# Token mixer products over the whole array, one bank at a time, in an attention and mixer kernel

## The chip, the cores and the metric

The kernel runs on one core of one Trainium2 chip. The metric is the device time of one execution in microseconds (us); lower is better. A measurement is the median of several executions.

## The reference

Eight batches of causal attention with a decay (8 heads, 576 positions, 64 values per head), whose output feeds a token mixer (two products along the positions) and a channel mixer (two products along the 512 channels), each with a ReLU between and with the input added back:

```python
decay = cum[:, :, :, None] - cum[:, :, None, :]          # cum = cumsum(log(f))
scores = np.where(causal, -1e9, q @ k.T / 8 + decay)
x = softmax(scores) @ v                                  # [8, 576, 512]
h = np.maximum(x.transpose(0, 2, 1) @ w_tok1, 0.0) @ w_tok2   # w_tok1 [576, 256], w_tok2 [256, 576]
u = x + h.transpose(0, 2, 1)
out = u + np.maximum(u @ w_ch1, 0.0) @ w_ch2             # w_ch1 [512, 1536], w_ch2 [1536, 512]
```

The weights come in double precision and are decoded in the kernel. A factor is kept as a high and a low part (names ending in h and l, both fp32r), and a product is the sum of three: high by high, low by high, high by low.

## The kernel before

The program is a list of 4,680 steps. Each step is a group of instructions on one engine (PE has 940 of them), with the buffers that it needs. Tables of numbers (`ORDER`, one for each of PE, DVE, ACT, POOL and the DMA queue SP) say in which order an engine gets its steps. A planner replays them with costs for each step to give out buffers; the order of an engine is that of its table. All engines run in order and wait for each other with semaphores.

There are two stages. In the attention stage the 32 pairs of heads are worked through, and after each half of a batch (16 halves in all) the token mixer of that half. Meanwhile DVE, ACT and POOL decode the weights of the channel mixer, which go out to DRAM. The channel stage that follows is 2,520 matmuls in five chunks of two times 464 or 456 columns (`WIDE`), each over all 128 rows and columns of TensorE.

The attention stage uses TensorE in parts. Scores (L745, L751) and the products with v (L889, L892) run on 64 rows by 64 columns, four at a time side by side. Transposes (L860 of the probabilities, L1260 of the attention output) run on 64 rows by 128 columns, two side by side: even heads on the upper 64 rows, odd heads on the lower. PSUM has eight banks; two row halves never write into one bank at the same time.

The token mixer (`mixer`) of a half batch does, on PE: 20 transposes (L1260); two steps of the first product (`t1`, moving tiles of 256 columns); then for each of two groups of 128 channels two steps of the second product (`tok2`, moving tiles of 288 columns). ACT and DVE read the results out of the banks, take the ReLU and split into high and low (tiles `ring`), and DVE adds the second product to `xt`. The products are made by `joint`: a matmul over 128 rows is cut into two over 64 rows, which run side by side and write into two banks (L1243). Step (phase) 0 gives rows 0 to 63 to bank 0 and rows 64 to 127 to bank 1; phase 1 swaps the banks and adds the other half. Between the phases a `nop` on PE waits for the last matmuls of phase 0:

```python
for z in (0, 1):
    p.op("PE", [hm(width[0])] * n, lambda z=z: phase(z), rd=rd, wr=ps, bufs=[*ps, *extra], mode=1, ...)
```

So there are 96 such steps: 32 of the first product (14 pairs of matmuls, of which one may lack its second half) and 64 of the second (6 pairs). The names below: `xn`, `t1h`, `t1l`, `t2h`, `t2l` and `ring` are operands of these products, `pr` the probabilities, `ux`, `sg` and `wq` operands of the channel stage (L1045 to L1047 and L1126 to L1128).

A DMA of the attention stage is held back until an earlier one has landed (`run`, `hold`), so that the DMAs after that one, up to the last before it, amount to at least `AHEAD` in the planner's time (4,500, at 300 bytes a unit for most, 235 and 247 for some).

Of the kernel before, what the change touches and what calls it, by code (L numbers as in the profile page):

```python
# [15 lines left out]
P = 128  # L16
# [8 lines left out]
AHEAD, AHEAD_TO = 4500.0, 8  # L25
# [42 lines left out]
    ),  # L68
    DVE=(
# [193 lines left out]
class Plan:  # L263
# [48 lines left out]
    def run(self, slots):  # L312
# [6 lines left out]
        for k, o in enumerate(sent):  # L319
            if k > 1:  # L320
                ahead += sent[k - 1].lat
# [1212 lines left out]
```

## Time and profile before

| | |
|---|---|
| median of 3 executions | 933.82 us (933.11 to 934.39) |
| profiled execution | 933.73 us, span 931.9 us |
| PE busy | 911.5 us (98%), 10270 matmuls |
| DVE, ACT, POOL busy | 709.0, 523.0, 234.8 us |
| moved by DMA | 242.49 MB, 260 GB/s |
| granted TensorE clock | 0.999 |

The span goes from the first to the last instruction; the profiled execution took 1.8 us more. "Busy" of PE counts the time in which at least one matmul is on its way. Matmuls overlap, so a matmul's own duration is not what it costs; what it costs is the distance from its start to that of the next.

### The profile page before, as it was taken

How to read it: one execution, taken by the hardware profiler on the slowest of the kernel's cores; microseconds unless marked ns; L12 is line 12 of the kernel's file. 1: busy time of each engine (PE TensorE's matmuls, PEld its weight loads, DVE VectorE, ACT ScalarE, POOL GpSimd, SP SyncE). 2: the span in 40 equal slices, each digit the busy share in tenths (PEclk: the TensorE clock that was granted, in tenths of full speed). 3: DMA queues.
4: the chain of work that ended last, by engine and by line, in shares of the span. 5: the costliest groups of instructions: out<-in, count | busy, mean ns of one | idle time of the engine just before them, and what ended most of it. 6: DMA issues, size and time to landing. Idle time of an engine off the chain costs nothing.

```text
span 931.9 us, 26826 instructions
## 1 busy us (share of the span) xinstructions
PE 911.5 (98%) x10270; PEld 794.3 (85%) x10270; DVE 709.0 (76%) x1894; ACT 523.0 (56%) x1340; POOL 234.8 (25%) x320
## 2 busy tenths in 40 slices
PE   7999899999999999999999999999999999999998
PEld 5678788888788888988888888888889999999997
DVE  7988878888788778664898369953898359954786
ACT  6979888999888989721463135512353125421242
POOL 4577567676675662100000000000000000000000
PEclk9999999999999999999999999999999999999999
DMA  8989989899998988469799888898879878887774
GB/s 247 250 277 287 308 210 321 290 297 264 301 301 251 288 265 252 134 205 329 237 308 286 269 234 236 261 302 258 261 248 287 275 227 250 248 270 232 241 249 153
DMA packets 145023, 242.49 MB, mean 260 GB/s; under 512 B 19136, under 2 KB 76736, under 8 KB 144896
## 3 DMA queue, kind: packets, MB, share of 16 engines
q1 hardware_dynamic: 144800, 240.64, 84.0%
q8 instruction: 81, 1.33, 0.6%
q14 instruction: 46, 0.38, 0.1%
q10 hardware_dynamic: 96, 0.15, 0.0%
HBM read 199.52 MB, written 41.21 MB: 258 GB/s over the span
## 4 chain that ended last, share of the span: by engine, by line
PE 89%; DVE 6%; DMA 2%; ACT 2%; issue 2%; SPq 0%; DVEq 0%; ACTq 0%
PE bank L1243 11%; PE bank L1045 9%; PE bank L1126 9%; PE bank L1127 9%; PE bank L1128 9%; PE bank L1046 9%; PE bank L1047 9%; PE bank L745 7%; PE bank L889 7%; PE bank L860 5%; DVE pr L786 3%; PE bank L1260 1%; ACT pr L790 1%; DVE pf L868 1%; DMA d_raw<-in_w_tok 1%
## 5 line engine op out<-in xcount | busy, mean ns | idle before, releaser
L487 ACT ACTIVATE st<-H 128x464 fp32r<-128x464 f32 (+1 forms) x210 | 120.7, 587 | 117.4 <-PE bank L1127 78.1
L790 ACT ACTIVATE pr<-pr,nmin 128x192 f32<-128x192 f32 (+4 forms) x320 | 176.5, 558 | 15.2 <-DVE nmin L786 14.9
L1126 PE MATMUL bank<-st,wq 128*128 128x464 f32 (+1 forms) x420 | 156.0, 371 | 0.0
L1127 PE MATMUL bank<-st,wq 128*128 128x464 f32 (+1 forms) x420 | 155.9, 371 | 0.0
L1128 PE MATMUL bank<-st,wq 128*128 128x464 f32 (+1 forms) x420 | 155.7, 371 | 0.0
L786 DVE CUSTOM_DVE_ANT_0 pr<-bank,cb 128x448 f32<-128x448 f32 (+3 forms) x260 | 108.6, 458 | 11.3 <-PE bank L751 6.7
L745 PE MATMUL bank<-raw 64*64 64x448 f32 (+6 forms) x1408 | 111.4, 397 | 5.4 <-issue 1.8
L496 DVE TENSOR_TENSOR st<-H,st 128x464 fp32r<-128x464 f32 (+1 forms) x150 | 92.3, 631 | 13.4 <-ACT st L487 13.3
L981 DVE TENSOR_TENSOR tmp<-bank,tmp 128x464 f32<-128x464 f32 (+1 forms) x80 | 50.3, 633 | 61.6 <-PE bank L1047 46.6
L889 PE MATMUL bank<-pf,vr 64*64 64x128 f32 (+3 forms) x2048 | 96.5, 315 | 0.0
L870 ACT ACTIVATE pf<-bank 128x512 f32<-128x512 f32 x152 | 84.0, 595 | 11.8 <-PE bank L860 6.3
L1128 PEld LDWEIGHTS bank<-st,wq 128*128 128x128 f32 x420 | 78.8, 188 | 9.2
L1126 PEld LDWEIGHTS bank<-st,wq 128*128 128x128 f32 x420 | 78.9, 188 | 9.0
L1127 PEld LDWEIGHTS bank<-st,wq 128*128 128x128 f32 x420 | 78.8, 188 | 8.8
L889 PEld LDWEIGHTS bank<-pf,vr 64*64 64x64 f32 x2048 | 75.2, 133 | 7.7 <-ACT pf L870 1.5
L745 PEld LDWEIGHTS bank<-raw 64*64 64x64 f32 x1408 | 54.5, 133 | 31.7 <-issue 9.8
L1071 ACT ACTIVATE H<-bank 128x464 f32<-128x464 f32 (+1 forms) x30 | 16.5, 555 | 115.2 <-PE bank L1047 109.3
L860 PE MATMUL bank<-ident,pr 64*128 64x64 f32 x1536 | 63.6, 224 | 4.3 <-issue 1.4
L860 PEld LDWEIGHTS bank<-ident,pr 64*128 64x128 f32 x1536 | 58.9, 139 | 8.1 <-DVE nmin L786 2.2
L920 POOL TENSOR_TENSOR xt<-xt,rb 128x64 f32<-128x64 f32 (+1 forms) x64 | 52.4, 837 | 48.0 <-DMA rb<-recd 26.0
L790 ACT ACTIVATION_READ_ACCUMULATOR pr<-pr,nmin 128x1 f32 (+1 forms) x320 | 62.5, 195 | 0.0
L1243 PE MATMUL bank<-t2h,ring 64*128 64x288 f32 x512 | 60.7, 304 | 1.8 <-issue 1.5
(166 smaller groups left out, 2072.8 us busy)
## 6 DMA issues: line engine op xcount, KB each, us to landing
wq<-wd SPq DMA_DIRECT2D x420, 256.0 KB
raw<-in_qk SPq DMA_DIRECT2D x32, 576.0 KB
cb<-decd SPq DMA_DIRECT2D x26, 576.0 KB
d_raw<-in_w_ch SPq DMA_DIRECT2D x48, 256.0 KB
wd<-sg SPq DMA_DIRECT2D x24, 512.0 KB
vr<-in_v SPq DMA_DIRECT2D x64, 160.0 KB
rb<-recd SPq DMA_DIRECT2D x32, 320.0 KB
wd<-sg SPq DMA_DIRECT2D x24, 384.0 KB
```

The costliest lines, as they stand in the source:

```text
L487: nc.scalar.activation(out, in_, func, scale=scale)
L496: nc.vector.tensor_tensor(out, in_, asf(hi), op=ALU.subtract)
L745: nc.tensor.matmul(at(buf)[HALF[h], of : of + n], q[:, i0 : i0 + D], k[:, j0 : j0 + n], start=t not in (0, 1), stop=not nd, skip_group_che ...
L786: nc.vector.tensor_tensor_reduce(o, x, y, -1.0 / D**0.5, c0[:m, NS + z : NS + z + 1] if t == 5 else 3e38, op0=ALU.add, op1=ALU.min, accum_ ...
L790: nc.scalar.activation(x, x, AF.Exp, bias=E["nmin"][sm][:m, t : t + 1], scale=-1.0, accum_out=E["rec"][rm][:m, c : c + 1])
L860: nc.tensor.transpose(at(ps[s])[:, k * D : (k + 1) * D], at(pr)[r, x, :, :].rearrange("p a b -> p (a b)"), E["ident"][r, r])
L870: p.op("ACT", d_act(512), lambda src_=src_, o=o: nc.scalar.activation(o(), src_(), AF.Copy), rd=[ps[s]], wr=[(pt, s)], bufs=[ps[s], pt])
L889: nc.tensor.matmul(at(av[z])[o, 256 - w : 256], at(vr)[r, vblk(j), :], at(pt)[r, c : c + w], start=j == 4, stop=gi == 2, skip_group_check= ...
L1126: nc.tensor.matmul(o, wt[:, 0, :], h_, start=(first and x == 0), stop=False, skip_group_check=True)
L1127: nc.tensor.matmul(o, wt[:, 1, :], h_, start=False, stop=False, skip_group_check=True)
L1128: nc.tensor.matmul(o, wt[:, 0, :], l_, start=False, stop=(x == FX - 1), skip_group_check=True)
L1243: last[s] = nc.tensor.matmul(at(ps[s ^ z])[:, : width[0]], a, m, start=(z == 0 and i == 0), stop=(z == 1 and i == len(todo[s]) - 1), skip_ ...
```

## The change

The two steps of a product are no longer phases over row halves but the two banks: each step (`half`) runs its matmuls over all 128 rows into one bank, with no wait between the steps, and each holds only its own bank. The first product has one more matmul, whose unwanted rows are filled with zeros once on POOL. The planner is told that these steps have the array shape of the channel stage. The hold of DMAs counts bytes (1,200,000) in place of planned time. The five tables of order are new in the attention stage (one line of each version is shown); the last 362 steps of PE are in the same order as before.

```diff
-AHEAD, AHEAD_TO = 4500.0, 8
+AHEAD, PACED = 1200000, 8
 ORDER = dict(
     PE=(
-        "14:12 145 135:2 146 26:2 155 139 28:3 185 156 140 31:11 202 188 42 193 43:6 165 168 171 49 275 267 284 218 174 "
+        "14:12 145 135 146 136 26:2 139 155 28:3 140 185 156 31:10 193 202 41:7 188 48:2 165 168 171 267 275 284 218 174 "
...
-            if k > 1:
-                ahead += sent[k - 1].lat
-            while j + 1 < k - 1 and ahead - sent[j + 1].lat >= AHEAD:
+            ahead += sent[k - 1].size if k else 0
+            while j + 1 < k - 1 and ahead - sent[j + 1].size >= AHEAD:
                 j += 1
-                ahead -= sent[j].lat
-            if j >= 0 and o.at_sp:
+                ahead -= sent[j].size
+            if j >= 0 and o.paced:
...
+        def low_():
+            lo_pool(lo(), asf(tl()[2]), hi())
+            if tok == ("t1", 0):
+                nc.gpsimd.memset(asf(lo()[T0:]), 0.0)
...
     def joint(ps, terms, width, rd, extra):
-        last = {}
-
-        def phase(z):
-            todo = [list(terms(s ^ z, s)) for s in (0, 1)]
-            if z:
-                E["after"](*last.values())
-            for i in range(max(len(x) for x in todo)):
-                for s in (0, 1):
-                    if i < len(todo[s]):
-                        a, m = todo[s][i]
-                        last[s] = nc.tensor.matmul(at(ps[s ^ z])[:, : width[0]], a, m, start=(z == 0 and i == 0), stop=(z == 1 and i == len(todo[s]) - 1), skip_group_check=True)
-
-        for z in (0, 1):
-            n = width[1]
-            p.op("PE", [hm(width[0])] * n, lambda z=z: phase(z), rd=rd, wr=ps, bufs=[*ps, *extra], mode=1, **({} if z else {"lat": 250}))
+        def half(x):
+            todo = list(terms(x))
+            for i, (a, m) in enumerate(todo):
+                nc.tensor.matmul(at(ps[x])[:, : width[0]], a, m, start=i == 0, stop=i == len(todo) - 1, skip_group_check=True)
+
+        for x in (0, 1):
+            p.op("PE", [mm_(width[0])] * width[1], lambda x=x: half(x), rd=rd, wr=[ps[x]], bufs=[ps[x], *extra])
```

The first place is the first product of the program, on PE. Before, the matmuls alternate between banks 66 and 70, each over 64 rows; the piece is where phase 0 ends, and transposes (L860) come between it and phase 1 (the last row).

```order
L860 MATMUL bank_69<-ident,pr_191 128x64
L1243 MATMUL bank_66<-xn_196,t1h 128x256
L1243 MATMUL bank_70<-xn_196,t1h 128x256
...
L1243 MATMUL bank_66<-ring_146,t1h 128x256
L1243 MATMUL bank_70<-ring_146,t1h 128x256
L1243 MATMUL bank_66<-ring_146,t1l 128x256
L860 MATMUL bank_63<-ident,pr_191 128x64
L860 MATMUL bank_64<-ident,pr_191 128x64
...
L1243 MATMUL bank_70<-xn_196,t1h 128x256
```

In the changed kernel, at the same product, all transposes stand ahead of it, and bank 67 follows bank 63 at once (L1240 is the line of these matmuls there, L864 the transposes, L749 the scores):

```order
L864 MATMUL bank_69<-ident,pr_191 128x64
L1240 MATMUL bank_63<-xn_196,t1h 128x256
...
L1240 MATMUL bank_63<-ring_146,t1h 128x256
L1240 MATMUL bank_63<-ring_146,t1l 128x256
L1240 MATMUL bank_67<-xn_196,t1h 128x256
...
L1240 MATMUL bank_67<-ring_146,t1h 128x256
L1240 MATMUL bank_67<-ring_146,t1l 128x256
L749 MATMUL bank_64<-raw_180 64x448
```

What moved is the group of transposes, from between the two steps to ahead of both; the product's neighbours are steps of 64 rows on both sides.

The second place is the end of the attention stage, where the last products stand between steps of the channel stage (L1045 to L1047 before, L1049 to L1051 in the changed kernel). Before, on PE, the last transposes follow one phase of a second product and the other phase follows them:

```order
L1047 MATMUL bank_67<-sg_158,wq_168 128x464
L1243 MATMUL bank_63<-t2h,ring_147 128x288
L1243 MATMUL bank_64<-t2h,ring_147 128x288
...
L1260 MATMUL bank_65<-ident,xt_145 128x64
...
L1243 MATMUL bank_64<-t2h,ring_148 128x288
L1243 MATMUL bank_63<-t2h,ring_148 128x288
L1045 MATMUL bank_66<-ux_161,wq_169 128x464
```

In the changed kernel the same place reads:

```order
L1051 MATMUL bank_67<-sg_158,wq_168 128x464
L1240 MATMUL bank_63<-t2h,ring_147 128x288
...
L1240 MATMUL bank_64<-t2h,ring_148 128x288
L1256 MATMUL bank_65<-ident,xt_145 128x64
...
L1256 MATMUL bank_69<-ident,xt_145 128x64
L1049 MATMUL bank_70<-ux_161,wq_169 128x464
L1240 MATMUL bank_65<-t2h,ring_147 128x288
```

Here a product follows a step of the channel stage and both use the array alike; the transposes are now the only steps of another shape.

## Rows read from the trace of the kernel before

**Rows 1.** Page, part 1: busy time, share of the span, instructions.

```profile
PE 911.5 (98%) x10270; PEld 794.3 (85%) x10270; DVE 709.0 (76%) x1894; ACT 523.0 (56%) x1340; POOL 234.8 (25%) x320
```

**Rows 2.** Busy time by stage: stretch, length, engines (instructions), clock, DMA share, GB/s.

```profile
0.00:52.00 52.00, 43.45 (x759) 30.29 (x761) 45.83 (x187) 39.12 (x116) 28.29 (x51) 1.00 0.87 262
52.00:390.00 338.00, 329.85 (x6849) 282.51 (x6847) 281.72 (x1025) 295.73 (x876) 204.18 (x268) 1.00 0.89 270
405.00:932.00 527.00, 523.25 (x2506) 468.61 (x2502) 375.83 (x671) 184.21 (x340) 0.00 (x0) 1.00 0.82 255
```

**Rows 3.** The same view, two stretches of the channel stage.

```profile
600.00:700.00 100.00, 100.00 (x476) 88.94 (x475) 69.44 (x124) 34.79 (x64) 0.00 (x0) 1.00 0.86 265
800.00:900.00 100.00, 100.00 (x484) 90.62 (x483) 65.87 (x117) 31.15 (x58) 0.00 (x0) 1.00 0.82 251
```

**Rows 4.** Timeline of PE, 392 to 400 us: start, length, what, how many.

```profile
392.42 0.37 PE L1046 MATMUL bank<-sg,wq 128*128 128x464 f32 x1
392.63 0.37 PE L1047 MATMUL bank<-sg,wq 128*128 128x464 f32 x1
392.93 0.40 PE L1243 MATMUL bank<-t2h,ring 64*128 64x288 f32 x2
393.17 0.30 PE L1243 MATMUL bank<-t2l,ring 64*128 64x288 f32 x2
393.30 0.43 PE L1243 MATMUL bank<-t2h,ring 64*128 64x288 f32 x4
...
395.17 0.29 PE L1243 MATMUL bank<-t2h,ring 64*128 64x288 f32 x2
395.39 0.48 PE L1045 MATMUL bank<-ux,wq 128*128 128x464 f32 x1
395.71 0.37 PE L1046 MATMUL bank<-ux,wq 128*128 128x464 f32 x1
...
398.38 0.29 PE L1243 MATMUL bank<-ring,t1h 64*128 64x256 f32 x2
398.51 0.28 PE L1243 MATMUL bank<-ring,t1l 64*128 64x256 f32 x1
398.85 0.39 PE L1243 MATMUL bank<-xn,t1h 64*128 64x256 f32 x2
399.07 0.28 PE L1243 MATMUL bank<-xn,t1l 64*128 64x256 f32 x2
399.19 0.40 PE L1243 MATMUL bank<-xn,t1h 64*128 64x256 f32 x4
399.43 0.28 PE L1243 MATMUL bank<-xn,t1l 64*128 64x256 f32 x2
```

**Rows 5.** Timeline of PE, 87 to 90 us (four steps of two second products, interleaved).

```profile
87.10 0.29 PE L1243 MATMUL bank<-t2l,ring 64*128 64x288 f32 x2
...
90.02 0.35 PE L1243 MATMUL bank<-t2h,ring 64*128 64x288 f32 x2
```

**Rows 6.** Timeline of PE at four pauses: in brackets the idle time before, and its releaser.

```profile
101.72 0.46 PE L1260 MATMUL bank<-ident,xt 64*128 64x64 f32 x8 [1.78 <-issue]
...
115.66 0.48 PE L745 MATMUL bank<-raw 64*64 64x320 f32 x4 [1.36 <-issue]
...
122.66 0.40 PE L1243 MATMUL bank<-t2h,ring 64*128 64x288 f32 x1 [1.48 <-issue]
...
291.86 0.53 PE L860 MATMUL bank<-ident,pr 64*128 64x64 f32 x10 [1.36 <-issue]
```

**Rows 7.** Page, part 3: a DMA queue, packets, MB, share of 16 engines.

```profile
q8 instruction: 81, 1.33, 0.6%
```

More of the change, by code (lines that the diff above doesn't have):

```diff
@@ L259 @@
 class Op:
-    __slots__ = ("eng", "dur", "head", "tail", "lat", "fn", "bufs", "need", "outs", "ready", "start", "idx", "port", "mode", "hold", "at_sp", "got")
+    __slots__ = ("eng", "dur", "head", "tail", "lat", "fn", "bufs", "need", "outs", "ready", "start", "idx", "port", "mode", "size", "hold", "paced", "got")
 class Plan:
@@ L282, in op @@
         o = Op()
-        o.mode, o.hold, o.at_sp = mode, None, self.batch < AHEAD_TO
+        o.mode, o.size, o.hold, o.paced = mode, 0, None, self.batch < PACED
         o.port = (port or eng == "POOL") and self.batch >= PORT
@@ L317, in run @@
         assert sorted(o.idx for q in queue.values() for o in q) == list(range(len(self.ops)))
-        j, ahead, sent = -1, 0.0, queue["SP"]
+        j, ahead, sent = -1, 0, queue["SP"]
         for k, o in enumerate(sent):
-            if k > 1:
-                ahead += sent[k - 1].lat
-            while j + 1 < k - 1 and ahead - sent[j + 1].lat >= AHEAD:
+            ahead += sent[k - 1].size if k else 0
+            while j + 1 < k - 1 and ahead - sent[j + 1].size >= AHEAD:
                 j += 1
-                ahead -= sent[j].lat
-            if j >= 0 and o.at_sp:
+                ahead -= sent[j].size
+            if j >= 0 and o.paced:
                 o.hold = sent[j]
@@ L482, in dma @@
     def dma(fn, nbytes, **k):
-        return p.op("SP", k.pop("dur", 475), fn, lat=nbytes / k.pop("rate", 300), **k)
+        o = p.op("SP", k.pop("dur", 475), fn, lat=nbytes / k.pop("rate", 300), **k)
+        o.size = nbytes
+        return o
     def hi_act(out, in_, scale=1.0, func=AF.Copy):
@@ L600, in decode @@
         p.op("POOL", d_pts(w), lambda: hi_pool(hi(), asf(tl()[2])), rd=[gb], wr=[(tok, "h")], bufs=[gb])
-        p.op(
-            "POOL", d_ptt(w), lambda: lo_pool(lo(), asf(tl()[2]), hi()),
-            rd=[gb, (tok, "h")], wr=[(tok, "l")], bufs=[gb], port=True,
-        )
+        def low_():
+            lo_pool(lo(), asf(tl()[2]), hi())
+            if tok == ("t1", 0):
+                nc.gpsimd.memset(asf(lo()[T0:]), 0.0)
+        p.op("POOL", d_ptt(w) + 250 * (tok == ("t1", 0)), low_, rd=[gb, (tok, "h")], wr=[(tok, "l")], bufs=[gb], port=True)
     def hi_(out, in_, **k):
@@ L1282, in mixer, with t1 @@
     hb, lb = Buf("ring"), Buf("ring")
-    def t1(x, s):
-        r, ks = HALF[s], slice(x * P, (x + 1) * P)
+    def t1(x):
+        ks = slice(x * P, (x + 1) * P)
         for t in range(1, NS):
             ms = slice((t - 1) * W, t * W)
-            yield E["t1h"][r, t, ks], at(xn)[r, 0, ms]
-            yield E["t1l"][r, t, ks], at(xn)[r, 0, ms]
-            yield E["t1h"][r, t, ks], at(xn)[r, 1, ms]
-        yield E["t1h"][r, 0, ks], at(x0)[r, :W]
-        if not s:
-            yield E["t1l"][r, 0, ks], at(x0)[r, :W]
+            yield E["t1h"][:, t, ks], at(xn)[:, 0, ms]
+            yield E["t1l"][:, t, ks], at(xn)[:, 0, ms]
+            yield E["t1h"][:, t, ks], at(xn)[:, 1, ms]
+        yield E["t1h"][:, 0, ks], at(x0)[:, :W]
+        yield E["t1l"][:, 0, ks], at(x0)[:, :W]
     joint(
@@ L1306, in tok2, with terms @@
         cs = [slice(k * W + (c % HC) * P, k * W + (c % HC + 1) * P) for k in range(NT)]
-        def terms(x, s):
-            r, ss = HALF[s], slice(x * HS, (x + 1) * HS)
+        def terms(x):
+            ss = slice(x * HS, (x + 1) * HS)
             for k in range(NT):
-                yield at(hb)[r, cs[k]], E["t2h"][r, k, ss]
-                yield at(hb)[r, cs[k]], E["t2l"][r, k, ss]
-                yield at(lb)[r, cs[k]], E["t2h"][r, k, ss]
+                yield at(hb)[:, cs[k]], E["t2h"][:, k, ss]
+                yield at(hb)[:, cs[k]], E["t2l"][:, k, ss]
+                yield at(lb)[:, cs[k]], E["t2h"][:, k, ss]
         joint(
```

397 rows, old and new, of tables (ACT, DVE, PE, POOL) are left out of this document.

## The prediction

> **What bounds the kernel now.** I read the busy times first, then the stages, then the timeline of PE. PE is busy for 98% of the span, DVE for 76%, ACT for 56% [rows 1]. By stage, PE is busy for 329.85 of the 338 us from 52 to 390, which is the steady part of the attention stage, and for 523.25 of the 527 us after 405, the channel stage [rows 2]. The reader is to see that PE runs through both stages nearly without idle time, while in the steady part DVE (281.72) and ACT (295.73) are close behind. The channel stage is not touched (the last 362 steps of PE keep their order), so the time changes by what the attention stage changes, and that by what PE has to do in it and how long it stands still. It stands still for 8.2 us of the steady part (338 less 329.85), and four pauses alone are 1.78 + 1.36 + 1.48 + 1.36 = 6.0 us of that [rows 6]. Only some 2 us are left as plain waits for other engines; more is hidden in starts that come late inside what counts as busy.
>
> **Term 1, the matmuls themselves.** A pair over 64 rows costs 0.12 us at 256 columns (start to start: 399.19 to 399.43 is two pairs) and 0.1327 at 288 columns (87.10 to 90.02 is 22 pairs) [rows 4, 5]. So before there are 32 x 14 x 0.12 + 64 x 6 x 0.1327 = 53.8 + 51.0 = 104.8 us of pairs. After, the same numbers of matmuls (448 and 384) run one by one over the whole array. The trace has such matmuls only at 464 columns (100 us / 476 = 0.2101 us) and at 456 (100 / 484 = 0.2066) [rows 3]. At the granted clock of 1.00, which is 2.4 GHz, the columns alone take 0.1933 and 0.19, so each matmul costs 17 ns beyond its columns; a pair costs 13 ns beyond (0.12 less 0.1067, and 0.1327 less 0.12). The two ends: if the 17 ns are the same at any width, a matmul costs 0.1237 at 256 and 0.137 at 288 columns, 108.0 us in all (+3.2); if they shrink with the columns (8.7%), it costs 0.116 and 0.1304, 102.0 us (-2.8). I take 15 ns, between the two fixed costs that rows show: 0.1217 and 0.135, so 54.5 + 51.8 = 106.3, or **+1.5 us**. It is nearer to the upper end because the pairs' 13 ns are the same at both of their widths.
>
> **Term 2, changes of the array's shape.** Counted in the order of PE's 940 steps, neighbours of unlike shape (64x64, 64x128, 128x128) go from 118 to 157. At the products: before, 24 of the 96 steps are entered and 10 left with a change; 35 are entered from transposes, which have their shape. After, 37 runs of products are entered and 37 left with a change, since nothing else in the attention stage but a few warm-up matmuls and the first steps of the channel stage uses the whole array. What one costs is in the rows: from the channel stage to a product, the last matmul takes 0.30 in place of 0.21, and the product's first pair 0.24 in place of 0.13, together 0.20 us; back again, 0.22 for 0.13 and 0.32 for 0.21, also 0.20 [rows 4]. The rows do not show a change between the whole array and scores or transposes. The ends are 0.10, when only one of the two delays is paid (+3.9 us), and 0.32, which is what the drain and restart between two phases costs where it comes with a wait (398.51 to 399.07 is 0.56, evenly it would be 0.24; +12.5 us) [rows 4]. I take 0.195, since both changes in the rows cost that: 39 x 0.195 = **+7.6 us**. The Trainium skill, in TensorEngine Tiling (Array Packing), section Tiling Modes, states that "Changing tiling mode (not just tile) drains the TensorE"; it gives no price, and it speaks against this change, which moves the products out of the mode of their neighbours. The trace agrees with it in 392.63 to 392.93. If only the number of columns in use counted, and not the rows, the term would be 0.
>
> **Term 3, what goes away.** Steps that follow transposes or their own other phase start slowly even without a change of shape: 0.22 us for a first pair against 0.12 [rows 4]. For the 35 steps entered from transposes this is about 0.085 net, as the first pair begins while the last transposes are still running: -3.0 us, because the price of a change in term 2 has it in already. The wait between phases: at its worst, with nothing between the phases, the last single matmul is followed after 0.34 us in place of 0.12 [rows 4]; where two products are interleaved, nothing is lost between phases at all, 22 pairs running evenly [rows 5]. 37 products' steps follow one another directly; between 0 and 0.22 each, I take 0.07, nearer to the interleaved case, which is the usual one: -2.5 us. Together **-5.5 us**, with ends of -3 and -11.
>
> **Term 4, the pauses.** The four pauses lie inside groups of like instructions, and the trace names no engine and no DMA as what ended them, only "issue" [rows 6]. I read them as PE running out of instructions: the instruction queue moves 81 packets, 1.33 MB [rows 7], and 2 x 10270 instructions [rows 1] in 81 packets are 254 each, or 65 bytes an instruction. Its packets share the DMA engines, busy for 0.89 of the steady part [rows 2], with the bulk. After, PE has 800 matmuls and as many weight loads fewer, 6 packets of 81, and the bulk in flight is held to 1.2 MB where it was 1.35 MB for most DMAs (4,500 x 300). That makes a pause less likely but does not remove its cause: a tenth of 6 us, **-0.6 us**; the ends are -6.0 (all go) and +3.0 (two more).
>
> **The rest.** The memset on POOL comes once in the first 52 us, where POOL is busy for 28.29 [rows 2]; its cover is the wait of the first product for its other operands, and uncovered it is one POOL instruction, and those of that stretch take 28.29 / 51 = 0.55 us on average: 0, at most 0.6. Less in flight could delay a load: 1.2 MB at 270 GB/s are 4.4 us of backlog in place of 5.0; I take 0, since PE waits for no bulk load in the rows above, and hold 1 us as the bound. The new orders of the other engines move their work with that of PE; DVE and ACT stay at 83% and 87% of the steady part [rows 2] and can win or lose what PE now waits: 0, with the 2 us of plain waits on either side, and in the first 52 us, with 8.55 us idle [rows 2], as much again.
>
> **Sum.** +1.5 + 7.6 - 5.5 - 0.6 = +3.0 us. The span becomes 934.9, the profiled execution 936.7 (span and 1.8 around it); that execution lay 0.09 below the median of 933.82, so **936.8 us**.
>
> **The rivals.** (A) *No change that can be told* (within 0.2%, 1.9 us, about what a measurement of this kernel can tell from no change). The whole-array matmuls shrink with their columns (102.0 in place of 106.3, -4.3): 936.8 - 4.3 = 932.5. For it: the 8 columns between 464 and 456 cost 3.5 ns, their share at 8.7% over the clock being 3.6 and without it 3.3, which does not tell the two apart [rows 3]. Against it: the pairs' fixed 13 ns.
> (B) *Faster: the pauses go.* 800 matmuls and a shorter backlog are enough for the instruction packets to come in time: -6.0 in place of -0.6, so 931.4. It decides once more than 4.9 us of the 6.0 are gone, that is when at least all but one pause are. For it: one of the four lies in a product, where half of the instructions go. Against it: the other three lie in scores or transposes, which stay as they are.
> (C) *Faster: the whole array needs no fixed cost at these widths.* Columns alone would be 448 x 0.1067 + 384 x 0.12 = 93.9 us, -12.4 against term 1: 924.4. Against it: 17 ns at 476 and 484 matmuls in rows 3. The Trainium skill, in TensorE: Matmul & The Clock Gate, section Back-to-back issue gap, gives the columns over 2.4 GHz plus 2.5 ns for a warm array; by that estimate the products would take 95.9 us and the time would be 926.4. The trace differs from it at 464 columns (0.2101 us, by the page 0.1958).
> (D) *Much slower.* Changes cost 0.26, halfway to the upper end: 39 x 0.065 = +2.5, and two pauses more (2 x 1.5, in place of the -0.6): +3.6, so 942.9. For it: changes between scores and products, which no row here prices.
>
> **How the numbers follow.** The forecast (slower by 2 to 7 us) has 0.43; A 0.25; B 0.18; C 0.04; D 0.10. The predicted time is the forecast's, 936.8; its own range is 935.7 to 940.5. Over all cases the range is 931.0 to 941.5: it takes in A, nearly all of B, and the lower part of D. Faster (under 931.95) is B and C, 0.22; the same is A, 0.25; slower is the forecast and D, 0.53.
>
> **What would show it.** In the changed kernel's timeline: a product's matmuls 0.122 and 0.135 us apart (term 1), 0.2 us lost on entering and leaving a run of products (term 2), nothing lost between the two steps of a product (term 3), three to five pauses with "issue" inside a group (term 4), and 75 instruction packets in all. The channel stage must take the same 527 us. The prediction is wrong if the distance of whole-array matmuls falls below 0.117, if the pauses are gone or doubled, or if the steady part has another 5 us of waits for ACT or DVE in it that the new orders brought or took.

## The result, and the profile after

The changed kernel takes 942.01 us (median of 6 runs, 939.42 to 944.68) against 934.11 for the kernel before beside it (6 runs): a ratio of 1.0078, with an interval of 1.0054 to 1.0101. On 933.82 us that is 941.1, or +7.3 us. The forecast was +3.0: the direction held, the size did not, and the terms that made the difference were not the ones that the forecast was about.

The profiled execution took 944.68 us. Its page, part 1 (busy us, share of the span, instructions), and part 3 (the queue of [rows 7]):

```profile
PE 922.0 (98%) x9470; PEld 795.2 (84%) x9470; DVE 714.6 (76%) x1894; ACT 522.9 (55%) x1340; POOL 238.1 (25%) x321
...
q8 instruction: 75, 1.23, 0.5%
```

The stages, as in [rows 2]:

```profile
0.00:52.00 52.00, 45.24 (x696) 30.97 (x698) 43.35 (x172) 35.61 (x105) 23.11 (x43) 0.93 0.75 225
52.00:390.00 338.00, 327.64 (x5936) 272.67 (x5930) 281.95 (x1023) 291.54 (x872) 211.60 (x275) 1.00 0.90 272
405.00:943.00 538.00, 534.09 (x2589) 478.26 (x2587) 380.87 (x682) 186.96 (x347) 0.00 (x0) 1.00 0.82 255
```

The span ends 11 us later. PE's last 362 steps take 460.1 us from the first start to the last end where they took 459.8, so the channel stage has not changed: it only starts later, and all of the loss is in the attention stage. There PE is less busy than before (327.64 of 338 us, before 329.85), although it runs 800 matmuls fewer: it waits more. The first 52 us have a granted clock of 0.93, which belongs to this one execution (below).

A product in the timeline of PE, to be read against [rows 4, 5]:

```profile
91.24 0.40 PE L1240 MATMUL bank<-t2h,ring 128*128 128x288 f32 x1
91.47 0.29 PE L1240 MATMUL bank<-t2l,ring 128*128 128x288 f32 x1
91.61 0.42 PE L1240 MATMUL bank<-t2h,ring 128*128 128x288 f32 x2
...
94.25 0.29 PE L1240 MATMUL bank<-t2l,ring 128*128 128x288 f32 x1
94.39 0.29 PE L1240 MATMUL bank<-t2h,ring 128*128 128x288 f32 x1
94.61 1.58 PE L864 MATMUL bank<-ident,pr 64*128 64x64 f32 x44
...
112.00 0.28 PE L1240 MATMUL bank<-xn,t1l 128*128 128x256 f32 x1
...
115.12 0.28 PE L1240 MATMUL bank<-ring,t1l 128*128 128x256 f32 x1
```

Within the run, 91.47 to 94.39 is 22 matmuls, 0.1327 us each; 112.00 to 115.12 is 26, 0.120 each. These are the pairs' numbers to the third digit. The first matmul after scores takes 0.23 in place of 0.133, and the last before transposes 0.22: 0.10 and 0.09 us more. The rows of the channel stage had a delay on both sides of a change. Here the last transposes ahead of a product are also late, by some 0.1 us, but the step behind a product starts no later than behind any other change. So a run of products costs about 0.3 us, where the forecast counted two changes of 0.195.

What PE waits for between 52 and 400 us (line, releaser: us in total, times, longest):

```profile
PE bank L749 <- ACT pf L874: 2.2, 2, 2.0
PE bank L864 <- ACT pf L874: 1.3, 6, 0.2
PE bank L864 <- DVE xn L498: 1.1, 1, 1.1
PE bank L893 <- DVE xt L1317: 1.1, 1, 1.1
PE bank L1240 <- DVE ring L501: 0.7, 1, 0.7
...
```

All the rows of this view add up to 9.0 us for other engines and nothing for "issue". For the kernel before the same view gives 1.4 us for other engines and 6.8 us for "issue", the pauses of [rows 6] among them. The pauses are gone, and waits of about the same size have come. The longest, in PE's timeline:

```profile
198.87 1.21 PE L864 MATMUL bank<-ident,pr 64*128 64x64 f32 x32
200.32 0.27 PE L864 MATMUL bank<-ident,pr 64*128 64x64 f32 x1 [0.23 <-ACT pf L874]
200.83 0.71 PE L864 MATMUL bank<-ident,pr 64*128 64x64 f32 x15 [0.24 <-ACT pf L874]
203.54 1.72 PE L749 MATMUL bank<-raw 64*64 64x448 f32 x16 [2.00 <-ACT pf L874]
```

and on ACT:

```profile
201.66 0.57 ACT L874 ACTIVATE pf<-bank 128x512 f32<-128x512 f32 x1
202.14 0.44 ACT L794 ACTIVATE pr<-pr,nmin 128x192 f32<-128x192 f32 x1
...
202.91 1.06 ACT L874 ACTIVATE pf<-bank 128x512 f32<-128x512 f32 x2
```

The third group of transposes (x1 and x15) waits twice for copies of the earlier ones, and then the scores (L749) stand for 2.00 us until ScalarE has made the first of the two copies that begin at 202.91, behind exponentials (L794): PE, ACT and PE again run one after the other, where they should overlap.

To add this up, I took each of PE's steps between the first product of mixer 1 and that of mixer 15, its start to the next step's start, less what such a step takes by itself (for matmul steps of a product the distances above, for others the usual value before a step of its own shape). The steps by themselves are 285.0 or 285.1 us in each kernel of this table; what lies beyond is sorted by size. "Pauses" are gaps over 0.9 us inside a step; small losses count up to 0.25 us of each step, long waits what is above:

| kernel | changes of shape there | small losses | long waits | pauses | stretch, us |
|---|---|---|---|---|---|
| before | 84 | 26.0 | 2.8 | 7.2 | 321.1 |
| changed | 123 | 31.5 | 10.9 | 0.9 | 328.4 |
| changed products, old orders (below) | 160 | 33.8 | 2.9 | 0 | 321.7 |
| changed, 16 steps moved (below) | 123 | 30.8 | 4.2 | 0 | 320.1 |
| old orders, grouped (below) | 118 | 36.4 | 25.4 | 3.0 | 349.8 |

The changed kernel is 7.3 us longer in the stretch: +5.5 small losses, +8.1 long waits, -6.3 pauses.

### The profile page after: what moved, and what is told of

It reads as the page before. It is cut to its first block, busy times and chain, and to the rows that moved or that the text cites. A ratio compares the mean times of both kernels' runs of the same rounds, so it can differ in the third digit from the quotient of the medians.

```text
span 942.9 us, 25223 instructions
## 1 busy us (share of the span) xinstructions
PE 922.0 (98%) x9470; PEld 795.2 (84%) x9470; DVE 714.6 (76%) x1894; ACT 522.9 (55%) x1340; POOL 238.1 (25%) x321
## 4 chain that ended last, share of the span: by engine, by line
PE 83%; DMA 5%; ACT 5%; DVE 5%; issue 1%; POOL 0%; SPq 0%; DVEq 0%; ACTq 0%; POOLq 0%
PE bank L1130 9%; PE bank L1131 9%; PE bank L1049 9%; PE bank L1132 9%; PE bank L1240 9%; PE bank L1051 9%; PE bank L1050 9%; PE bank L749 6%; PE bank L893 6%; PE bank L864 4%; ACT pr L794 2%; DVE pr L790 2%; ACT pf L874 1%; DMA raw<-in_qk 1%; DMA d_raw<-in_w_ch 1%
## 5 line engine op out<-in xcount | busy, mean ns | idle before, releaser
L794 ACT ACTIVATE pr<-pr,nmin 128x192 f32<-128x192 f32 (+4 forms) x320 | 176.4, 557 | 22.0 <-DVE nmin L790 19.3
L749 PE MATMUL bank<-raw 64*64 64x448 f32 (+6 forms) x1408 | 114.0, 402 | 3.4 <-ACT pf L874 2.7
L893 PE MATMUL bank<-pf,vr 64*64 64x128 f32 (+3 forms) x2048 | 99.7, 319 | 1.7 <-DVE xt L1317 1.1
L749 PEld LDWEIGHTS bank<-raw 64*64 64x64 f32 x1408 | 54.2, 134 | 32.1 <-issue 10.8
L864 PE MATMUL bank<-ident,pr 64*128 64x64 f32 x1536 | 62.2, 228 | 5.2 <-ACT pf L874 1.3
L864 PEld LDWEIGHTS bank<-ident,pr 64*128 64x128 f32 x1536 | 54.2, 140 | 14.6 <-issue 3.4
L924 POOL TENSOR_TENSOR xt<-xt,rb 128x512 f32<-128x512 f32 (+1 forms) x64 | 51.8, 829 | 50.5 <-DMA rb<-recd 24.0
L1061 ACT ACTIVATE tmp<-bank 128x464 f32<-128x464 f32 (+1 forms) x30 | 16.5, 552 | 84.2 <-PE bank L1051 84.2
L794 ACT ACTIVATION_READ_ACCUMULATOR pr<-pr,nmin 128x1 f32 (+1 forms) x320 | 62.2, 194 | 0.0
```

Of the source, the lines that this page charges most:

```text
L749: nc.tensor.matmul(at(buf)[HALF[h], of : of + n], q[:, i0 : i0 + D], k[:, j0 : j0 + n], start=t not in (0, 1), stop=not nd, skip_group_che ...
L794: nc.scalar.activation(x, x, AF.Exp, bias=E["nmin"][sm][:m, t : t + 1], scale=-1.0, accum_out=E["rec"][rm][:m, c : c + 1])
L864: nc.tensor.transpose(at(ps[s])[:, k * D : (k + 1) * D], at(pr)[r, x, :, :].rearrange("p a b -> p (a b)"), E["ident"][r, r])
L893: nc.tensor.matmul(at(av[z])[o, 256 - w : 256], at(vr)[r, vblk(j), :], at(pt)[r, c : c + w], start=j == 4, stop=gi == 2, skip_group_check= ...
```

## The experiments

Theories. **S**: the loss is the price of the changes of shape. **O**: the new orders of the engines bring it, whatever the products cost. A sharper form of O is **W**: the new orders make TensorE wait for copies that come late. A third candidate was the hold of the transfers (**H** in two of the expectations). All ratios are to the kernel before on the same chip.

**whole_old_order.** The changed products in the orders (all engines) and with the hold of the kernel before: 196 changes of shape in place of 157.

```diff
-AHEAD, PACED = 1200000, 8
+AHEAD, PACED = 4500.0, 8
...
-            while j + 1 < k - 1 and ahead - sent[j + 1].size >= AHEAD:
+            while j + 1 < k - 1 and ahead - sent[j + 1].lat >= AHEAD:
...
 ORDER = dict(  # the tables of the kernel before
```

> Whole-array products with the five order tables and the hold of DMAs of the kernel before. PE then has 196 neighbours of unlike shape (before 118, changed kernel 157). Theory S (changes of the array's shape are what costs): 78 more changes at 0.15 to 0.195 us are +11.7 to +15.2, less 5.5 for slow starts and waits between phases that go away: 6 to 10 us slower than before (ratio 1.006 to 1.011), that is as slow as the changed kernel or slower. Rival O (the new orders cost the time, not the products): within 2 us of before (ratio 0.998 to 1.002).

Measured: 937.18 us (10 runs), 1.0046 (1.0028 to 1.0065). The ratio lies between the ranges of O and S and in neither. With 39 changes more than the changed kernel it is not slower than that one, which S alone cannot explain. Its row in the table has the reason for the stretch: 7.8 us of small losses for 76 changes, 0.10 each, no new long waits, and the pauses gone, so that it is only 0.6 us longer there. The loss in its profile lies ahead of the stretch: the first product of mixer 1 starts 3.5 us later than before, after a wait of 1.87 us for a load of values at 44.7 us and a granted clock of 0.73 from 52 to 56 us. Whether every execution has that is not known, so what makes up the 3.9 us of the median is not settled.

**whole_time_hold.** The changed kernel with the hold counted in planned time again (the same lines of the hold as above, the new tables kept).

> The changed kernel with the hold of DMAs counted in planned time (4500) as before. Theory S: the hold is not what moved the time; within 2 us of the changed kernel (ratio to before 1.005 to 1.010), and no pause over 1.2 us with 'issue' inside a group of like instructions, as in the changed kernel, since there are fewer instructions. Rival H (the hold in bytes is what removed the pauses): pauses come back, three to five of 1.3 to 2 us, and the time rises by 4 to 8 us over the changed kernel (ratio 1.012 or more).

Measured: 940.01 us (6 runs), 1.0072 (1.0049 to 1.0096). The hold does not make the loss. The pauses do not come back either: "issue" is 1.2 us between 52 and 400.

**pairs_bytes_hold.** The kernel before with the hold counted in bytes, 1,200,000.

```diff
-AHEAD, AHEAD_TO = 4500.0, 8
+AHEAD, AHEAD_TO = 1200000, 8
...
-            while j + 1 < k - 1 and ahead - sent[j + 1].lat >= AHEAD:
+            while j + 1 < k - 1 and ahead - sent[j + 1].size >= AHEAD:
```

> The kernel before with the hold of DMAs counted in bytes (1,200,000). Theory S: pauses stay (three to five), time within 2 us of before. Rival H: the four pauses of 6 us go, and the time falls by 4 to 6 us (ratio 0.9935 to 0.996).

Measured: 931.68 us (12 runs), 0.9984 (0.9962 to 1.0005). The hold alone changes nothing in the time that can be told; "issue" is down to 2.0 us in its one profile, in two pauses, so the three to five that S expected did not stay either.

**price_rows.** The kernel before, where the second of the matmuls in 420 steps of the channel stage runs over 64 rows; half of that product is left out.

```diff
-nc.tensor.matmul(o, wt[:, 1, :], h_, start=False, stop=False, skip_group_check=True)
+nc.tensor.matmul(o, wt[:D, 1, :], h_[:D], start=False, stop=False, skip_group_check=True)
```

> The kernel before, where one matmul in three of the second half of the channel stage (the one of the low weights, L1127, 420 in all) runs over rows 0 to 63 only: half of that product is left out. Nothing else changes; PE is never idle there. Each of the 420 is entered and left with a change of shape, 840 changes. Theory S with the price of the trace (0.20 us a change): +168 us, about 1102; if the two delays of one change are shared by two changes that follow so closely, half of it, +84, about 1018. Rival (only the number of columns counts, or the change costs only with a wait for operands): within 5 us of before.

Measured: 1098.51 us against 933.26, +165.25 for 840 changes: **0.197 us for a change of rows**. In the timeline:

```profile
639.85 0.37 PE L1126 MATMUL bank<-st,wq 128*128 128x464 f32 x1
640.15 0.47 PE L1127 MATMUL bank<-st,wq 64*128 64x464 f32 x1
640.55 0.48 PE L1128 MATMUL bank<-st,wq 128*128 128x464 f32 x1
640.87 0.37 PE L1126 MATMUL bank<-st,wq 128*128 128x464 f32 x1
```

The three matmuls start 0.30, 0.40 and 0.32 us apart; three evenly would take 0.63 [rows 3], so two changes cost 0.39. Term 2's 0.195 is confirmed by itself for this place.

**price_cols.** The same, but the matmul keeps its 128 rows and writes 64 of its 128 output rows (half of that product is left out).

```diff
-nc.tensor.matmul(o, wt[:, 1, :], h_, start=False, stop=False, skip_group_check=True)
+nc.tensor.matmul(o[:D], wt[:, 1, :D], h_, start=False, stop=False, skip_group_check=True)
```

> The kernel before, in which the second matmul of each of the 420 steps that the earlier price run changed writes 64 of its 128 output rows only (128 rows of the array and 64 columns, where the earlier run used 64 rows and 128 columns); half of that product is left out. If a change of columns costs what a change of rows did (0.197 us, 165 us for 840 changes): about 1095 us. If only a change of rows stops the array: 931 to 935 us, level with the kernel before.

Measured: 934.92 us against 933.21, +1.7 for 840 changes, within what one run can tell: at 128 rows a change from 128 columns to 64 and back is free. In the timeline the rhythm stays at 0.21 us:

```profile
599.84 0.37 PE L1126 MATMUL bank<-st,wq 128*128 128x464 f32 x1
600.05 0.37 PE L1127 MATMUL bank<-st,wq 128*64 128x464 f32 x1
600.26 0.37 PE L1128 MATMUL bank<-st,wq 128*128 128x464 f32 x1
600.47 0.37 PE L1126 MATMUL bank<-st,wq 128*128 128x464 f32 x1
```

At 64 rows this does not hold. In the timeline of the kernel before, a product on 64 rows and 128 columns is followed by scores on 64 and 64; its last matmul takes 0.20 us where the one before it takes 0.12:

```profile
57.07 0.29 PE L1243 MATMUL bank<-ring,t1h 64*128 64x256 f32 x2
57.19 0.28 PE L1243 MATMUL bank<-ring,t1l 64*128 64x256 f32 x1
57.39 0.76 PE L745 MATMUL bank<-raw 64*64 64x320 f32 x8
```

The transposes show the same. From the ninth-last start of a group to the start of the next step they take 0.31 us (median) when more transposes follow, 0.40 when a step on 64 and 64 does, and in whole_old_order also 0.40 when a product over the whole array does. So in the attention stage a change of columns alone delays the end of a step as much as a change of rows.

**whole_again.** The changed kernel once more, with no edit.

> The changed kernel itself, for a second profile and more times beside the other runs on the same chip. Both theories: ratio about 1.008 (1.0054 to 1.0101 was measured). What it tells apart is which waits of the first profile belong to the order and which to one execution. Theory S+W (the new orders bring shape changes at 0.2 us and, besides, long waits of TensorE for copies of ScalarE and VectorE): the waits before the score product at 203 us (1.34 us, 2.0 us after it was due, for ScalarE's copy), at 228 us (1.03 us, VectorE) and at 32 us come again within 0.3 us. Rival N (these waits are chance, and the 7 us come from the changes alone): other places, or none over 1 us. The start-up, 5 us late in the first profile at a granted clock of 0.65 in 30 to 40 us, is expected to be level with the kernel before (within 1 us), since the run with the hold in planned time did not show it.

Measured: 942.71 us (5 runs), 1.0095 (1.0059 to 1.0131). Two of the three waits come again at the same steps, 2.0 us before the scores and 1.1 us for VectorE: they belong to the order. The third, at 32 us, is 0.5 us here, and the start-up is 2.3 us later than the kernel before, not level with it. What differs besides is where the clock fell. The windows of this run (length, then busy us of PE, PEld, DVE, ACT and POOL; the granted clock stands third from the end):

```profile
196.00:200.00 4.00, 1.99 (x48) 1.57 (x44) 1.40 (x3) 3.41 (x12) 4.00 (x4) 0.93 0.73 244
200.00:204.00 4.00, 3.53 (x30) 1.64 (x34) 1.24 (x5) 0.90 (x2) 1.29 (x2) 0.50 0.98 246
204.00:208.00 4.00, 4.00 (x88) 3.14 (x84) 2.08 (x12) 2.11 (x7) 0.00 (x0) 0.72 0.53 204
```

and of the first profile:

```profile
28.00:32.00 4.00, 2.01 (x51) 1.49 (x45) 3.31 (x12) 1.90 (x8) 2.40 (x4) 0.94 0.89 280
32.00:36.00 4.00, 3.73 (x44) 2.93 (x44) 3.62 (x16) 1.59 (x4) 0.79 (x1) 0.50 0.72 232
36.00:40.00 4.00, 4.00 (x74) 2.96 (x74) 2.73 (x11) 3.56 (x12) 1.23 (x2) 0.71 0.39 99
...
200.00:204.00 4.00, 1.53 (x28) 0.95 (x25) 0.69 (x1) 3.96 (x13) 4.00 (x4) 1.00 0.89 250
204.00:208.00 4.00, 4.00 (x104) 2.92 (x100) 3.03 (x14) 1.44 (x6) 0.14 (x1) 1.00 0.94 317
```

At 200 us both have the 2.00 us wait; in the first profile the clock stays at 1.00, in this one it falls to 0.50 (the 1.2 GHz level). In the first profile it fell at 32 us, after a wait of 1.86 us. By busy time and clock that fall cost an estimated 3.0 us (3.73 x 0.50 + 4.00 x 0.29), which accounts for the first profile's late start-up: 5.0 us at the first product of mixer 0 against 2.3 here.

**whole_old_grouped.** The run with the old orders, but on PE the steps of one product that stood within six places of each other follow one another (33 steps moved): 154 changes in place of 196.

```diff
 PE (one of the places, step numbers):
- 376 467 526 377 527
+ 376 377 467 526 527
```

> The changed products with the orders and the hold of the kernel before, but the steps of one mixer product that stood within six places of each other on TensorE are pulled together (33 steps moved, 154 changes of shape instead of the 196 of the run with the old orders). Theory S (each change costs 0.2 us): 42 fewer changes take 6 to 8 us off the run with the old orders, ratio 0.996 to 0.999 to the kernel before, so no slower than it. Rival W (what pulling together saves in changes it gives back in waits for steps that are now asked for too early, as in the changed kernel): no better than the run with the old orders, 1.004 to 1.008, with waits of over 0.5 us at the pulled steps.

Measured: 964.2 us (6 runs), 1.0331 (1.0297 to 1.0364). S's forecast fails by over 30 us; W's fails by over 20, though the long waits that it named are there. PE's waits between 52 and 430 us:

```profile
PE bank L752 <- ACT pf L877: 3.8, 8, 1.0
PE bank L1243 <- DVE xn L501: 3.4, 3, 2.2
PE bank L867 <- DVE xn L501: 2.7, 2, 1.9
PE bank L867 <- ACT pf L877: 1.8, 5, 0.8
```

(The lines are numbered three higher here: L1243 is a product's matmul, L752 the scores, L867 the transposes.) In the table, small losses at changes fall from 24.2 to 18.7 us, 0.13 for each change saved, as S has it; 8.1 us of small and 22.5 us of long waits come in their place. Fewer changes are worth something, and orders that ask too early cost several times that.

**pairs_900k.** The kernel before with a hold of 900,000 bytes (`AHEAD, AHEAD_TO = 900000, 8`).

> The kernel before, pairs and orders as they were, with the hold of transfers counted in bytes, at 900,000 instead of the change's 1,200,000. Theory I (the four pauses of the kernel before come from instructions that reach TensorE late when big transfers run beside them): with less in flight the pauses are fewer, one or none, ratio 0.993 to 0.997. Rival (the pauses come with the number of instructions, whatever is in flight): two to four pauses, ratio 0.998 to 1.002, as with 1,200,000 (0.9984).

Measured: 941.65 us (8 runs), 1.0088 (1.0056 to 1.012). "Issue" falls to 0.7 us, but PE now waits 14.7 us for others: 4.7 us of it for loads of values (vr), 3.3 for GpSimd's xt. So the pauses nearly went, as theory I of the expectation said, but the time rose: 0.9 MB in flight is too little here.

**whole_moved.** The test of W: the changed kernel with 16 moves of one to four places (one is of eight, which the expectation passes over) in VectorE's and GpSimd's tables, mostly of steps that decode weights. They were searched with the program's own plan. TensorE's table, and with it all 157 changes of shape, is as in the changed kernel. Two of the places (step numbers):

```diff
 POOL:
- 2395 2406 2396 2391 2397 2424 2410 2408
+ 2395 2406 2391 2396 2410 2397 2424 2408
 DVE:
- 1660 2601 1667 1866 1877
+ 1660 1866 2601 1667 1877
```

> The changed kernel with 16 moves of one to four places in the tables of VectorE and GpSimd (mostly steps that decode weights, against copies that free banks); TensorE's table, and so its 157 changes of shape, and the hold are untouched. Theory W (the new orders make TensorE wait for copies that come late: about 9 us of waits for other engines between 52 and 400 us in the changed kernel, which the kernel before hardly has): 5 to 12 us off the changed kernel, ratio 0.995 to 1.004 to the kernel before. Rival S (the loss is the price of the changes of shape alone, of which there are as many): no gain, 1.006 to 1.010.

Measured: 934.22 us (12 runs), 1.0013 (0.9993 to 1.0032), which the changed kernel's interval does not touch. W holds: about 6 to 8 us of the loss go with nothing changed on TensorE's table. In the stretch of the table it is now 1.0 us shorter than the kernel before. PE's waits between 52 and 400 us add up to 4.7 us for other engines, from 9.0, and at the place of the 2.00 us wait there is none (lines two higher):

```profile
197.43 1.71 PE L866 MATMUL bank<-ident,pr 64*128 64x64 f32 x48
199.07 1.72 PE L751 MATMUL bank<-raw 64*64 64x448 f32 x16
```

Why this wait went is seen in the banks. The plan that reads the tables also hands out PE's banks, by the times at which it thinks them free. The instructions of PE there, the first two of each group of transposes, of the changed kernel and, below the dots, of this one (the first number is the place in PE's program, the name ahead of the arrow the bank):

```
2277 L864 MATMUL bank2_65<-ident_71,pr1_191 128x64
2278 L864 MATMUL bank3_66<-ident_71,pr1_191 128x64
2293 L864 MATMUL bank6_69<-ident_71,pr1_191 128x64
2294 L864 MATMUL bank7_70<-ident_71,pr1_191 128x64
2309 L864 MATMUL bank2_65<-ident_71,pr1_191 128x64
2310 L864 MATMUL bank7_70<-ident_71,pr1_191 128x64
...
2277 L866 MATMUL bank2_65<-ident_71,pr1_191 128x64
2278 L866 MATMUL bank3_66<-ident_71,pr1_191 128x64
2293 L866 MATMUL bank1_64<-ident_71,pr1_191 128x64
2294 L866 MATMUL bank5_68<-ident_71,pr1_191 128x64
2309 L866 MATMUL bank0_63<-ident_71,pr1_191 128x64
2310 L866 MATMUL bank4_67<-ident_71,pr1_191 128x64
```

In the changed kernel the third group of transposes goes to banks 2 and 7, which the first two groups have just filled, so it must wait for their copies. Here each group has banks of its own. So the moves act in part through the banks that the plan gives out, and what the moved steps themselves do and what the banks do was not separated.

**whole_searched** and **pairs_searched.** The byte hold, and orders of all engines searched with the plan from those of the kernel before, by many small moves: 185 changes of shape with the whole array, 135 with pairs.

> Whole-array products with the byte hold of the change, and orders searched anew from those of the kernel before on all engines, for few waits: 185 changes of shape, 28 more than the changed kernel. Theory W with S (waits of the order and changes at about 0.15 to 0.2 us both count, and the search takes waits off): 5 to 11 us under the run with the old orders, ratio 0.993 to 0.999. Rival S alone: 28 more changes than the changed kernel, so slower than it by 4 to 6 us, ratio over 1.010.

> The products as they were (pairs of 64 rows), with the byte hold and orders searched in the same way: 135 changes of shape. Theory W with S (the order decides, and pairs need fewer changes): under both kernels, ratio 0.985 to 0.996, and some 5 us under the whole-array products with searched orders. Rival P (pairs pay their instructions back in pauses of TensorE, 7 us in the kernel before, so that the whole array is the better one once orders are good): no lower than the whole-array run with searched orders.

Measured: 945.52 us (6 runs), 1.0138 (1.0103 to 1.0174), and 941.08 us (6 runs), 1.0097 (1.0063 to 1.013). Both expectations of W are missed. The whole array's time falls where S puts it, but its waits for others are 5.1 us and its stretch is 325.8 us, so it is no clean proof of S; the pairs' waits for others rose to 6.7 us. That a long search finds what the plan gets wrong is a guess that no run tests. P's condition is not met: with searched orders the median of the pairs is 4.4 us ahead, though the two intervals overlap.

**pairs_moved.** The kernel before with the byte hold and four moves of one to six places in VectorE's and GpSimd's tables.

> The products as they were (pairs of 64 rows) with the byte hold, the tables of TensorE, ScalarE and SyncE of the kernel before, and four moves of one to six places in those of VectorE and GpSimd. If mending late copies helps pairs as it helped the whole array: 2 to 6 us off the kernel before, ratio 0.994 to 0.998, and a version under both kernels. If the old tables have no waits worth mending (between 52 and 400 us the kernel before has about 3 us of waits for other engines over 0.2 us): ratio 0.997 to 1.001, as with the byte hold alone (0.9984), and the gap between whole-array products with mended tables (1.0013) and pairs stays at 0.3% or less.

Measured: 933.66 us (11 runs), 1.0024 (1.0004 to 1.0043). There is nothing to mend in the old tables, as the second case had it, though the ratio lies above its range of 0.997 to 1.001, which only the interval reaches. No version beats the kernel before by more than its interval.

## Why the prediction was right or wrong

**Term 1** (+1.5): the size was off. The matmuls of the whole array cost what the pairs cost, 0.120 and 0.1327 us, so 0. The fixed cost at 256 and 288 columns is the pairs' 13 ns, not the 17 ns of the channel stage.

**Term 2** (+7.6): the price of a change, 0.195 us, was right where it was read, in the channel stage (0.197 by itself). As one price for all 39 it was not: leaving a product cost about half of it, and so did the changes between 64x64 and 64x128, which differ in columns alone. Of the 118 changes before only 20 are changes of rows, of the 157 after 86; at 0.197 for these and nothing for the others the term would have been +13.0, or +7.5 together with term 3, and that is not the measured 5.5 either. That the array drains at a change of mode, as the Trainium skill has it in TensorEngine Tiling (Array Packing), section Tiling Modes, agrees with the delays of the runs at changes of rows, and of columns at 64 rows. At 128 rows a change of columns shows no such delay (price_cols, 0.002 us).

**Term 3** (-5.5; its second part is 37 x 0.07 = 2.6, so -5.6): with the price of term 2, too large a credit. Terms 2 and 3 together were to be +2.1; the small losses grew by 5.5 in the changed kernel, and by 4.8 once its long waits were mended. With the old orders a change cost 0.10 net; 39 at that rate are 3.9. How much of that is a lower price and how much slow starts that fell away is not parted.

**Term 4** (-0.6): the first step that failed. "A tenth of 6 us" was the wrong choice between the ends; the pauses went nearly all, -6.3 us, the end that rival B took. Instruction packets fell to 75, as said.

**The rest** (0): the second step that failed, and the larger. "The new orders of the other engines move their work with that of PE ... 0, with the 2 us of plain waits on either side" was argued from busy shares of 83% and 87%, and a busy share tells nothing of which copy comes late. The long waits rose by 8.1 us, and whole_moved took most of that back without touching PE's table. Both failed steps were named in the prediction's last paragraph as what would make it wrong.

The sum as measured in the stretch: 0 + 5.5 + 8.1 - 6.3 = 7.3, where the forecast had 1.5 + 2.1 + 0 - 0.6 = 3.0. That the direction came out right is in part luck: the two terms put at nearly nothing were large and almost cancelled (+8.1 and -6.3). It is chance, too, that the stretch of one profile gives the 7.3 us of the medians: that execution was 11 us longer than the profiled one before, and 4.1 us of it lie ahead of the stretch. **A** did not hold, nor **C**: the fixed cost is there. **B** was right that the pauses go (why, stays open, below) and wrong about the sign of the whole. **D** came close in size by the wrong way: a change does not cost 0.26, and there were no more pauses.

Two things stay open. Pairs in the new orders have no run: the two phases of a pair need both banks, and with these tables the plan finds no step that can start. And the cause of the pauses is not settled. "Issue" between 52 and 400 us is 4.7 to 6.8 us in three profiles of pairs with the hold in planned time, 0.7 to 3.0 in four with the hold in bytes, and 0 to 1.2 in seven of the whole array. Both fewer instructions and less in flight go with fewer pauses; that instructions came late is argued only, and the byte hold alone did not shorten the median by more than its interval.

## What to carry to other kernels

Where tables or a planner set the order, read what a change does to the waits for copies before the price of its instructions: here the price in the channel stage was known to 0.01 us, and the order decided. To part the two, run the new instructions in the old order and the new order with a few steps moved on the engines that wait least. A change of array shape costs something at every place priced here but one, 128 against 64 columns at 128 rows; so put work of like shape side by side, but don't move steps several places for it: what is asked for early is waited for.

## What the runs showed that was not expected

In the channel stage a change of rows costs 0.197 us and a change of columns none (0.002), at the same place and the same width. Between steps on 64 rows a change of columns does cost, about 0.09 us at the end of the step before it.

A wait of PE of about 2 us can cost more than itself: in whole_again the clock was at 0.50 from 200 to 204 and at 0.72 from 204 to 208, after PE had been busy for 1.99 of the 4 us before. By busy time and clock (3.53 x 0.50 + 4.00 x 0.28) that is an estimate of at most 2.9 us more. It does not follow each time: the same wait in the first profile left the clock at 1.00.

Moves in the tables of VectorE and GpSimd changed the banks in which TensorE's results lie, since one plan gives out both; so a table that is not TensorE's can put a wait on TensorE.
